# Linear-attention backward in a four-layer training step: feature derivative computed in place, and layer 0's key and value gradients transposed by DMA instead of TensorE

## The chip, the cores and the metric

The kernel runs on one core of a Trainium2 chip. The metric is the device time of one execution in microseconds (us), as the median of several executions. Before the change it is 2252.24 us, the median of 7 runs between 2244.93 and 2256.58 us. The profile below is of one further execution.

## What is computed

The reference is the forward pass and the gradients of four residual layers with sequence length 2048, width 640 and 32 heads of 20. Layers 0 and 2 are linear attention (A), layers 1 and 3 are sliding-window attention (B); the two A layers share their weights, and so do the two B layers. Cut to the part that the change touches:

```python
def _A_ref(x, wqkv, wo):                     # Dh = 20, H = 32
    qkv = (x @ wqkv).reshape(B, S, 3, H, Dh).transpose(2, 0, 3, 1, 4)
    q, k, v = qkv[0], qkv[1], qkv[2]
    phi = lambda t: jnp.where(t > 0, t + 1, jnp.exp(t)) + 1e-6
    pq, pk = phi(q), phi(k)
    kv = jnp.einsum("bhsd,bhse->bhde", pk, v)
    z = jnp.einsum("bhsd->bhd", pk)
    num = jnp.einsum("bhqd,bhde->bhqe", pq, kv)
    den = jnp.einsum("bhqd,bhd->bhq", pq, z)[..., None] + 1e-6
    o = num / den
    return o.transpose(0, 2, 1, 3).reshape(B, S, D) @ wo

x = x + _A_ref(_layernorm(x), A_wqkv, A_wo)
x = x + _B_ref(_layernorm(x), B_wqkv, B_wo)
x = x + _A_ref(_layernorm(x), A_wqkv, A_wo)
x = x + _B_ref(_layernorm(x), B_wqkv, B_wo)
_out, _vjp = jax.vjp(_f, A_x, A_wqkv, A_wo, B_wqkv, B_wo)
return (_out, *_vjp(grad_out))
```

The derivative of phi can be read off phi itself: for t > 0 it is 1, and for t <= 0 it is exp(t) = phi − 1e-6. So phi'(t) = min(phi − EPS, 1) with EPS = 1e-6. The backward pass keeps pq and pk from the forward pass and forms dq and dk by multiplying the gradient with respect to pq and pk by this derivative.

## The kernel before

The 2048 rows are worked on in 16 tiles of 128 rows (the partitions). Each tile has 640 columns, often taken as two halves of 320 (`CW`). The order of stages is: forward pass of the four layers; backward of layer 3's attention core; linear backward of layer 2 (about 1165 to 1285 us); backward of layer 1's core (to about 1750 us); then the weight gradients, which run to the end at 2253 us. The linear backward of layer 0 (about 1812 to 2037 us) is put amid the weight gradients.

The order of instructions on TensorE (PE), VectorE (DVE), ScalarE (ACT) and GpSimd (POOL) is the order in which the program issues them. It is written out by hand: each step of a tile has a slot number in the table `PLACES`, and all steps of all tiles are issued by rising slot. For the linear backward the list is `PLACES["l2"]`; tile t's step with offset a goes to slot 8t + a plus a base, so tiles follow each other at 8 slots. Layer 2 runs with nothing else in its slots but the ends of layer 3 and the beginning of layer 1. In layer 0 each slot ends with `fill(0.8)`, which issues some 0.8 us of weight-gradient matmuls. All DMAs are issued on SyncE's queue (SP), whose order the framework sets; at most 8 are under way, and an entry that waits for its data holds what stands behind it.

`plan_linear` (from L929) makes the steps of one tile. With their offsets:

- `load` (−10.4): for a pair of tiles, five DMAs, one of them `lpqk`, pq and pk beside one another (128 x 2 x 1280, bf16).
- `turn` dn (−1.3), v (0.6), pk (1.2): TensorE transposes the tile in six pieces of heads (`flip`, L162); DVE copies dn's result from PSUM (L167), ACT the others' (L165).
- `part`, two halves each of dn (1.9, 3.2), v (4.6, 6.2) and pk (7, 7.5): small products of the turned tile with the per-head matrices (L138) into a PSUM bank, `dense`. The result goes into `dqa`, a 128x1920 tile of dq, dk and dv. For dn (which gives dq) and v (which gives dk), DVE first computes `fd` = min(pq − EPS, 1), or that of pk, for 320 columns (L969), with one scalar_tensor_tensor and a constant tile `one`, and then multiplies the PSUM bank by it into dqa (L971). For pk (dv), ACT casts (L966).
- `turn_q` (5): dq is transposed into `dqT` by a DMA transpose (L978), in the first four tiles of layer 0 (`lp.by_pe` is 4 there, 0 in layer 2) by TensorE (`turn_pe`, L921).
- `turn_kv(1)` (8) and `turn_kv(2)` (8.3): dk and dv are transposed by five TensorE transposes each (L983); DVE copies dk's (L986), ACT dv's (L988) from PSUM to dqT. After the second, the whole of dqa is stored to `dqkv` in HBM; the weight gradients load it again as `rhs`.
- `dh(n, ci)` (10.2, 11.8, 14, 14.4, 15.4, 16): for each half ci, five products each of dqT's k, v and q part, in this order, with the transposed weights `WTA`, in one PSUM bank (`dense<-WTA,dqT`, L138); ACT then scales it into dh (L1001).
- `ln` (16.2) and `ln2` (18.7): layer norm backward: a DVE reduction (L1009), a small DVE op (L1011), an ACT op (L1018), and two POOL additions (L1012 with `lg`, L1019 into `lgn`). `lgn` is stored for each pair of tiles.

The weight gradients (`weight_jobs`, L1048 to L1110) keep a whole activation `lhs` (four DMA chunks of 640 KB) and slices of gradients `rhs` in SBUF; TensorE runs 32 matmuls per output piece (`wg`), which ACT (L1092) or DVE (L1094) casts to `wr`, stored by DMA. When the left operand changes, as late in the stage to `lhs<-o`, its chunks are loaded into buffers that have come free.

Of the kernel before, what the change touches and what calls it, by code (L numbers as in the profile page):

```python
# [11 lines left out]
ALU = mybir.AluOpType  # L12
AX = mybir.AxisListType
BF = mybir.dt.bfloat16
F32 = mybir.dt.float32
P = 128
D = 640
# [5 lines left out]
DT = D // P  # L23
# [10 lines left out]
CW = D // 2  # L34
LN_EPS = 1e-5
EPS = 1e-6
# [7 lines left out]
    f3=[-35.7, -30, -26.5, -25, -24, -23.8, -22.5, -18, -16.4, -14, -12.1, -7.4, -6.8, -6, -4.9, -3.5, -1.7, 11.3, 12.4, 13.4],  # L44
    bf=[2.1, 3.1, 5.2, 14.9, 17.9, 6.2, 7.8, 10, 14.6, 28.3],
    bh=[13.1, 14.5, 15.5, 17.1, 17.5, 18, 20, 21.2, 25.7, 28.3, 30, 36, 19.1, 20.1, 21.8, 22.5, 23.3, 24.6, 25.2, 27.5, 30.5, 31.7, 33, 35, 41.5, 43, 2.2, 8.3, 9.5, 12, 18.9, 34.5],
    l2=[-10.4, -1.3, 0.6, 1.2, 1.9, 3.2, 4.6, 6.2, 7, 7.5, 5, 8, 8.3, 10.2, 11.8, 14, 14.4, 15.4, 16, 16.2, 18.7],
    n1=[9.7, 0.5, 3.3, 3.6, 5.3, 9, 3, 4.7, 5.4, 5.6, 24],
    xx=[1, 1, 0, 0, 0, 0, 1, 1, 0, 0, 0, 0, 0, 1, 0, 0, 1, 0, 0, 0, 0, 0, 0, 1, 0, 0, 1, 0, 0, 0, 1, 0],
    bd=[0, 0, 1, 0, 0, 0, 1, 0, 0, 0, 0, 0, 0, 1, 1, 0, 0, 1, 1, 0, 1, 0, 1, 0, 1, 0, 1, 1, 0, 1, 1, 0])  # L50
# [2 lines left out]
class Kern:  # L53
    def __init__(self, ctx, tc, x0, A_w, A_wo, B_w, B_wo, grad, outs):
        self.ctx, self.tc = ctx, tc
        self.nc = nc = tc.nc
        self.W = dict(A=A_w, B=B_w)
        self.Wo = dict(A=A_wo, B=B_wo)
        self.grad = grad
        self.out_x4, self.out_gx, dWA, dWoA, dWB, dWoB = outs  # L60
        self.dW = dict(A=dWA, B=dWB)
        self.dWo = dict(A=dWoA, B=dWoB)
        self.serial = 0

        dram = ctx.enter_context(tc.tile_pool(name="dram", bufs=1, space=bass.MemoryType.DRAM))
        const = ctx.enter_context(tc.tile_pool(name="const", bufs=1))

        def d(name, shape, dt=BF):
            return dram.tile(shape, dt, name=name)

        self.hn = [d(f"hn{l}", [T, D]) for l in range(4)]
        self.dq = [d(f"dqkv{l}", [T, QT]) for l in range(4)]
        self.o = [d(f"o{l}", [T, D]) for l in range(4)]
        self.x2 = d("x2", [T, D])
        self.WTA, self.WoTB = d("WTAt", [P, NF * D]), d("WoTBt", [P, DT * D])
        self.x0 = x0
        self.gs = [d(f"g{l}", [T, D]) for l in range(3)] + [grad]
        self.sv = {}
        for l in (0, 2):
            self.sv[l] = dict(pqk=d(f"pqk{l}", [T, 2 * D]), v=d(f"v{l}", [T, DA]),  # L80
                              dn=d(f"dn{l}", [T, DA]))
        for l in (1, 3):
            self.sv[l] = {k: d(f"{k}{l}", [TT, P, 3, G * P]) for k in ("s", "T")}

        self.ident = const.tile([P, P], BF, name="ident")
        make_identity(nc, self.ident)
        self.bm = const.tile([KB, HB, HA], BF, name="bm")
        nc.gpsimd.memset(self.bm, 1.0)
        nc.gpsimd.affine_select(out=self.bm, in_=self.bm, compare_op=ALU.is_ge, fill=0.0, base=0,
                                pattern=[[-DH, HB], [0, HA]], channel_multiplier=1)  # L90
        nc.gpsimd.affine_select(out=self.bm, in_=self.bm, compare_op=ALU.is_ge, fill=0.0, base=DH - 1,
                                pattern=[[DH, HB], [0, HA]], channel_multiplier=-1)
        self.mhalf = const.tile([P, 1], F32, name="mhalf")
        nc.gpsimd.memset(self.mhalf, -0.5)
        self.rs = [const.tile([P, TT], F32, name=f"rs{l}") for l in range(4)]
        self.r = [const.tile([P, TT, H], F32, name=f"r{l}") for l in range(4)]
        self.mz = {l: const.tile([KB, 6, KA], BF, name=f"mz{l}") for l in (0, 2)}
        self.mzT = {l: const.tile([KA, 6, KB], BF, name=f"mzT{l}") for l in (0, 2)}
        self.one = const.tile([P, 1], BF, name="one")
        nc.gpsimd.memset(self.one, 1.0)  # L100
        self.dmz = const.tile([KB, 6, KA], BF, name="dmz")
        self.dmzT = const.tile([KA, 6, KB], BF, name="dmzT")
        self.macc = const.tile([KB, 6, KA], F32, name="macc")
# [823 lines left out]
    def plan_linear(self, st, lp, l, t, X, WT, g_out):  # L927

        nc = self.nc  # L929
        sv = self.sv[l]  # L930
        i = t % 2
        x = {}
# [9 lines left out]
        def src(nm):  # L942
            L = X[t // 2]
            return {"dn": L["dn"][:, i, :], "v": L["v"][:, i, :], "pq": L["pqk"][:, i, 0:D], "pk": L["pqk"][:, i, D:2 * D]}[nm]

        def turn(nm, K, cols, eng):
            x[nm] = self.flip(st.ps, lp.le, src(nm), nm + "T", K, 6, 0, eng, cols)

        def part(nm, c):
            if "dqkv" not in x:  # L950
                x["dqkv"] = lp.le.tile([P, QT], BF, name="dqa")
            tb, base = {"dn": (self.mzT[l], 0), "v": (self.dmzT, D), "pk": (None, 2 * D)}[nm]
            ps = st.ps.tile([P, 512], F32, name="dense", tag="m")
            jobs = []
            for h0, h1, j in ((0, 6, 0), (6, 12, 1), (12, 16, 2)) if c == 0 else ((16, 18, 2), (18, 24, 3), (24, 30, 4), (30, 32, 5)):
                out = ps[:, DH * (h0 - HALF * c):DH * (h1 - HALF * c)]
                if tb is not None:
                    rhs = tb[:, j, DH * (h0 - HS[j]):DH * (h1 - HS[j])]
                else:
                    rhs = self.dmz[:, j, :].rearrange("p (h d) -> p h d", d=HA)[:, h0 - HS[j]:h1 - HS[j], 0:DH]  # L960
                    out = self.heads(out)
                jobs.append((out, x[nm][:, j, :], rhs))
            self.banked(jobs)
            dst = x["dqkv"][:, base + c * CW:base + (c + 1) * CW]
            if nm == "pk":
                nc.scalar.copy(dst, ps[:, 0:CW])  # L966
            else:
                f = lp.le.tile([P, CW], BF, name="fd")
                nc.vector.scalar_tensor_tensor(out=f, in0=src("pq" if nm == "dn" else "pk")[:, c * CW:(c + 1) * CW], scalar=-EPS,  # L969
                                               in1=self.one.to_broadcast([P, CW]), op0=ALU.add, op1=ALU.min)  # L970
                nc.vector.tensor_tensor(out=dst, in0=ps[:, 0:CW], in1=f, op=ALU.mult)  # L971

        def turn_q():
            x["dT"] = st.sp.tile([P, NF, P], BF, name="dqT", bufs=3)
# [3 lines left out]
                self.dma(x["dT"][:, 0:DT, :], x["dqkv"][:, 0:D], transpose=True)  # L978

        def turn_kv(j):  # L980
            ps = st.ps.tile([P, 8, P], BF, name="flip", tag="m")
            for k in range(DT):
                nc.tensor.transpose(ps[:, k, :], x["dqkv"][:, j * D + k * P:j * D + (k + 1) * P], self.ident)  # L983
            o = x["dT"][:, j * DT:(j + 1) * DT, :]
            if j == 1:
                nc.vector.tensor_copy(o, ps[:, 0:DT, :])  # L986
            else:
                nc.scalar.copy(o, ps[:, 0:DT, :])  # L988
                self.dma(self.rows(self.dq[l], t), x["dqkv"])

        def dh(n, ci):
            if n == 0:
                x["ps"] = st.ps.tile([P, 512], F32, name="dense", tag="m")
                if ci == 0:
                    x["dh"] = st.sf.tile([P, D], F32, name="dh", tag="f")
                    x["ac"] = st.sm.tile([P, 2], F32, name="ac")
            k0 = (DT, 2 * DT, 0)[n]
            for k in range(k0, k0 + DT):
                self.mm(x["ps"][:, 0:CW], x["dT"][:, k, :], WT[:, k, ci * CW:(ci + 1) * CW], n == 0 and k == k0, n == 2 and k == k0 + DT - 1)
            if n == 2:  # L1000
                nc.scalar.activation(x["dh"][:, ci * CW:(ci + 1) * CW], x["ps"][:, 0:CW], ACT.Copy,  # L1001
                                     scale=self.rs[l][:, t:t + 1], accum_out=x["ac"][:, ci:ci + 1])
# [19 lines left out]
        a = PLACES["l2"]  # L1022
        fs = [lambda: turn("dn", KA, acols, nc.vector), lambda: turn("v", KA, acols, nc.scalar), lambda: turn("pk", KB, kcols, nc.scalar)]
        fs += [lambda nm=nm, c=c: part(nm, c) for nm in ("dn", "v", "pk") for c in range(2)]
        fs += [turn_q, lambda: turn_kv(1), lambda: turn_kv(2)]
        fs += [lambda n=n, ci=ci: dh(n, ci) for ci in range(2) for n in range(3)] + [ln, ln2]
        return ([(a[0], load)] if i == 0 else []) + list(zip(a[1:], fs))

    def linear_pools(self, left, side, by_pe):
# [382 lines left out]
```

The softmax here doesn't subtract the row's maximum and nothing guards it: scores larger than these inputs give would overflow.

## Time and profile before

| | |
|---|---|
| Median of 7 runs | 2252.24 us |
| Range of the runs | 2244.93 to 2256.58 us |
| Profiled execution, own time | 2254.7 us |
| Its span | 2253.0 us |
| Mean granted TensorE clock | 0.979 |
| Layer 2 tile period (starts of L1012) | 7.24 us |
| Layer 0 tile period (dqkv stores, 1863.43, 1876.57, ...) | 13.1 us |

The profile is of one execution. A group or timeline line names the source line, the engine, the operation and the result and inputs by the program's names, then the shapes; a bracket at the end of a timeline line tells how long the engine had been idle before it and what it waited for. "PEld" is the weight load of TensorE, which overlaps its matmuls, whose ends are modelled. In the chain of waits, each step is followed back to what released it. A row of the table of windows tells each engine's busy time in a stretch of the span. Rows of the page that give the setting, costliest groups of the two stages among them:

```profile
L138 PE MATMUL wg<-rhs,lhs 128*128 128x240 bf16 (+1 forms) x3840 | 375.3, 257 | 10.5 <-DMA lhs<-o 6.8
...
L1012 POOL TENSOR_TENSOR dh<-dh,lg 128x640 f32<-128x640 f32 x32 | 51.5, 1610 | 258.2 <-DVE s L1009 207.6
...
L138 PE MATMUL dense<-WTA,dqT 128*128 128x320 bf16 x960 | 161.5, 300 | 1.3 <-DMA dqT<-dqa 1.0
```

The columns after the shapes are the count, the busy time in us, the mean of one in ns, and the idle time before them with its main releaser. PE's idle time before the dh products in the whole span is 1.3 us, that before the weight gradients 10.5 us.

### The profile page before, as it was taken

The numbers are of one execution on the slowest core, as the hardware profiler recorded it, in microseconds if no ns is written. First come the engines' busy times: TensorE is split into PE (matmuls) and PEld (weight loads), VectorE is DVE, ScalarE is ACT, GpSimd is POOL, SyncE is SP. The second block draws the span as 40 slices with busy tenths as digits, with TensorE's granted clock in tenths as the row PEclk, the third lists the DMA queues.
The fourth block names the chain that finished last, engine by engine and source line by source line (L and its number), as shares of the span: only waits on it lengthen the run. The fifth ranks groups of instructions, "written<-read, shape, count | busy, mean of one in ns | idle before, by whom it ended". The sixth has DMA issues, their size and how long they took to land. (4 is left out here: it accounts for less than half of the span.)

```text
span 2253.0 us, 76829 instructions
## 1 busy us (share of the span) xinstructions
PE 2078.0 (92%) x32061; PEld 1693.0 (75%) x32061; DVE 1455.4 (65%) x2934; ACT 1356.7 (60%) x2109; POOL 1089.5 (48%) x1888
## 2 busy tenths in 40 slices
PE   7889998899989999998879899999998889999999
PEld 5667776577767877777767678777776788889998
DVE  6778885777744788887749858788776245550000
ACT  5467887377776888887736668788776234430000
POOL 2046665156666577777534456777774312220000
PEclk9999999999999999999989989999999999999999
DMA  7488875697879589998799733999987998857753
GB/s 260 141 238 227 226 223 150 165 222 218 206 210 230 150 182 209 210 215 178 164 280 260 200 88 106 199 207 211 198 191 165 270 290 244 255 161 199 201 143 90
DMA packets 721357, 449.50 MB, mean 200 GB/s; under 512 B 461296, under 2 KB 697840, under 8 KB 720624
## 3 DMA queue, kind: packets, MB, share of 16 engines
q1 hardware_dynamic: 721008, 444.58, 77.6%
q8 instruction: 251, 4.11, 0.8%
q14 instruction: 98, 0.80, 0.1%
HBM read 213.09 MB, written 149.82 MB: 161 GB/s over the span
## 5 line engine op out<-in xcount | busy, mean ns | idle before, releaser
L665 DVE TENSOR_TENSOR ds<-dp,e 128x768 bf16<-128x768 f32 (+2 forms) x512 | 464.1, 907 | 171.5 <-PE s L138 59.8
L662 ACT ACTIVATE e<-s 128x768 bf16<-128x768 f32 (+2 forms) x512 | 395.6, 773 | 138.0 <-PE s L138 102.7
L385 ACT ACTIVATE eT<-sT 128x1536 bf16<-128x1536 f32 (+2 forms) x256 | 350.8, 1370 | 131.5 <-PE sT L138 129.7
L138 PE MATMUL wg<-rhs,lhs 128*128 128x240 bf16 (+1 forms) x3840 | 375.3, 257 | 10.5 <-DMA lhs<-o 6.8
L138 PEld LDWEIGHTS <-lhs 128*128 128x128 bf16 x3840 | 338.1, 98 | 23.8 <-DMA lhs<-o 7.7
L674 POOL TENSOR_SCALAR_AFFINE_SELECT e<-e 128x256 bf16<-128x256 bf16 x512 | 207.2, 406 | 248.9 <-ACT e L662 244.1
L138 PEld LDWEIGHTS <-dqT 128*128 128x128 bf16 x1920 | 170.6, 98 | 62.9 <-issue 10.4
L391 POOL TENSOR_SCALAR_AFFINE_SELECT eT<-eT 128x512 bf16<-128x512 bf16 x256 | 162.2, 635 | 109.8 <-ACT eT L385 109.4
L138 PE MATMUL acc<-slabqs,ds 128*128 128x20 bf16 x2880 | 210.3, 172 | 1.4 <-ACT dq L744 0.5
L138 PE MATMUL dp<-slabvT,dT 32*128 32x384 bf16 (+2 forms) x1024 | 168.2, 321 | 45.0 <-DVE ds L665 39.8
L138 PE MATMUL acc<-ds,e 128*128 128x20 bf16 x2880 | 208.3, 172 | 0.0
L138 PEld LDWEIGHTS <-ds 128*128 128x128 bf16 x2880 | 187.9, 96 | 11.8 <-issue 3.5
L678 POOL TENSOR_SCALAR_AFFINE_SELECT e<-e 128x256 bf16<-128x256 bf16 x448 | 195.9, 437 | 0.0
L138 PEld LDWEIGHTS <-e 128*128 128x128 bf16 x2880 | 170.1, 96 | 10.6 <-issue 1.8
L1012 POOL TENSOR_TENSOR dh<-dh,lg 128x640 f32<-128x640 f32 x32 | 51.5, 1610 | 258.2 <-DVE s L1009 207.6
L685 PE MATMUL flip<-ident,ds 128*128 128x128 bf16 x1944 | 170.3, 222 | 3.3 <-DVE ds L772 1.2
L138 PE MATMUL s<-slabkT,slabqT 32*128 32x384 bf16 (+2 forms) x1024 | 168.2, 324 | 4.6 <-ACT dT L797 3.3
L1094 DVE CAST wr<-wg 128x240 bf16<-128x240 f32 (+1 forms) x72 | 27.2, 377 | 222.2 <-PE wg L138 219.9
L138 PE MATMUL dense<-WB,hnT 128*128 128x320 bf16 x960 | 166.2, 305 | 3.3 <-DVE o L459 2.2
L1092 ACT CAST wr<-wg 128x240 bf16<-128x240 f32 (+1 forms) x48 | 16.3, 339 | 254.0 <-PE wg L138 236.2
L138 PE MATMUL dense<-WTA,dqT 128*128 128x320 bf16 x960 | 161.5, 300 | 1.3 <-DMA dqT<-dqa 1.0
L138 PE MATMUL acc<-slabks,dsT 128*128 128x20 bf16 x2880 | 147.3, 172 | 10.8 <-DMA dsT<-ds 10.7
(176 smaller groups left out, 4606.4 us busy)
## 6 DMA issues: line engine op xcount, KB each, us to landing
rhs<-dqkv SPq DMA_DIRECT2D x64, 480.0 KB, 4.8
s<-s SPq DMA_DIRECT2D x32, 768.0 KB, 3.8
T<-T SPq DMA_DIRECT2D x32, 768.0 KB, 3.9
dqkv<-dq SPq DMA_DIRECT2D x16, 960.0 KB, 5.6
dqkv<-dqa SPq DMA_DIRECT2D x32, 480.0 KB, 4.6
slabkT<-T SPq DMA_DIRECT2D x56, 256.0 KB, 4.4
slabvT<-T SPq DMA_DIRECT2D x56, 256.0 KB, 3.7
slabks<-s SPq DMA_DIRECT2D x56, 256.0 KB, 3.7
```

Of the source, the lines that this page charges most:

```text
L138: return self.nc.tensor.matmul(out, lhsT=lhsT, rhs=rhs, start=start, stop=stop, skip_group_check=True, **kw)
L385: nc.scalar.activation(e[:, :, 0:nb * P], s[:, :, 0:nb * P], ACT.Exp)
L391: nc.gpsimd.affine_select(out=dg, in_=dg, compare_op=ALU.is_ge, fill=0.0, base=0, pattern=[[0, 4], [1, P]], channel_multiplier=-1)
L662: nc.scalar.activation(u.e[:, :, 0:u.cw], s[:, :, 0:u.cw], ACT.Exp)
L665: nc.vector.tensor_tensor(out=d.ds[:, :, 0:d.cw], in0=d.dp[:, :, 0:d.cw], in1=d.e[:, :, 0:d.cw], op=ALU.mult)
L674: nc.gpsimd.affine_select(out=dg, in_=dg, compare_op=ALU.is_ge, fill=0.0, base=0, pattern=[[0, 2], [-1, P]], channel_multiplier=1)
L678: nc.gpsimd.affine_select(out=fr, in_=fr, compare_op=ALU.is_ge, fill=0.0, base=-1, pattern=[[0, 2], [1, P]], channel_multiplier=-1)
L685: nc.tensor.transpose(ps[:, 3 * j + i, :], f.ds[:, j, i * P:(i + 1) * P], self.ident)
L1012: nc.gpsimd.tensor_tensor(out=x["dh"], in0=x["dh"], in1=L["g"][:, i, :], op=ALU.add)
L1092: nc.scalar.copy(o[:, 0:w], ps[:, 0:w])
L1094: nc.vector.tensor_copy(o[:, 0:w], ps[:, 0:w])
```

## The change

The constant `one` and the four `fd` ops per tile are gone. Instead two new steps per tile, `slope("pq")` at offset −2.3 and `slope("pk")` at offset 4.4, overwrite the loaded pq or pk of the tile (128x640, bf16) with min(x − EPS, 1) by one DVE tensor_scalar each; `part` then multiplies the PSUM bank by the overwritten tile directly. pq is read for nothing else here; pk's slope comes after its transposes at 1.2. This holds for both A layers: 128 `fd` ops go, 64 slopes come.

In layer 0 (`lp.by_pe` is 4), for tiles 4 to 15, `turn_kv` issues one DMA transpose of five 128x128 blocks for dk and one for dv on SP, in place of the ten TensorE transposes and the two copies; the store to `dqkv` is issued behind the second. For these tiles the offsets of the six dh steps, ln and ln2 are 5 larger. Layer 2 keeps its TensorE transposes. In the order of SP in layer 2, the transpose of dq of every other tile comes ahead of the load of lhn and the store of lgn; in layer 0 the new transposes stand among rhs and lhs loads and wr stores, and behind the last layer-0 tiles six chunks of `lhs<-o` instead of five are behind the wr store at 2063 us.

```diff
-        self.one = const.tile([P, 1], BF, name="one")
-        nc.gpsimd.memset(self.one, 1.0)
...
-    l2=[-10.4, -1.3, 0.6, 1.2, 1.9, 3.2, 4.6, 6.2, 7, 7.5, 5, 8, 8.3, 10.2, 11.8, 14, 14.4, 15.4, 16, 16.2, 18.7],
+    l2=[-10.4, -1.3, 0.6, 1.2, 1.9, 3.2, 4.6, 6.2, 7, 7.5, 5, 8, 8.3, 10.2, 11.8, 14, 14.4, 15.4, 16, 16.2, 18.7, -2.3, 4.4],
...
             if nm == "pk":
                 nc.scalar.copy(dst, ps[:, 0:CW])
             else:
-                f = lp.le.tile([P, CW], BF, name="fd")
-                nc.vector.scalar_tensor_tensor(out=f, in0=src("pq" if nm == "dn" else "pk")[:, c * CW:(c + 1) * CW], scalar=-EPS,
-                                               in1=self.one.to_broadcast([P, CW]), op0=ALU.add, op1=ALU.min)
-                nc.vector.tensor_tensor(out=dst, in0=ps[:, 0:CW], in1=f, op=ALU.mult)
+                nc.vector.tensor_tensor(out=dst, in0=ps[:, 0:CW], in1=src("pq" if nm == "dn" else "pk")[:, c * CW:(c + 1) * CW], op=ALU.mult)
+
+        def slope(nm):
+
+            nc.vector.tensor_scalar(out=src(nm), in0=src(nm), scalar1=-EPS, scalar2=1.0, op0=ALU.add, op1=ALU.min)
...
         def turn_kv(j):
+            if lp.by_pe and t >= 4:
+                self.dma(x["dT"][:, j * DT:(j + 1) * DT, :], x["dqkv"][:, j * D:(j + 1) * D], transpose=True)
+                if j == 2:
+                    self.dma(self.rows(self.dq[l], t), x["dqkv"])
+                return
...
-        fs += [lambda n=n, ci=ci: dh(n, ci) for ci in range(2) for n in range(3)] + [ln, ln2]
+        fs += [lambda n=n, ci=ci: dh(n, ci) for ci in range(2) for n in range(3)] + [ln, ln2, lambda: slope("pq"), lambda: slope("pk")]
+        if lp.by_pe and t >= 4:
+            a = a[:13] + [v + 5 for v in a[13:21]] + a[21:]
         return ([(a[0], load)] if i == 0 else []) + list(zip(a[1:], fs))
```

## The prediction

> **What bounds the kernel now.** I read the page first, then the chain of waits, then each stage that the edit touches in a table of windows, then one tile of it on the timeline. The page's totals and the chain by engine:
>
> ```profile
> PE 2078.0 (92%) x32061; PEld 1693.0 (75%) x32061; DVE 1455.4 (65%) x2934; ACT 1356.7 (60%) x2109; POOL 1089.5 (48%) x1888
> ...
> PE 20%; DMA 2%; SPq 1%; DVE 0%; ACT 0%; issue 0%; DVEq 0%; ACTq 0%
> ```
>
> TensorE (PE) is busy 92% of the span, and VectorE (DVE) hardly stands in the chain. But this edit touches only the two linear backward passes, so these decide. A row below gives the start, the length and the busy time of each engine, then the granted clock, the DMA share and GB/s: first layer 2, then layer 0 amid weight gradients, then the full-queue moment behind it.
>
> ```profile
> 1168.00:1283.00 115.00, 106.79 (x1219) 86.06 (x1219) 104.39 (x202) 75.50 (x152) 45.72 (x32) 0.96 0.82 229
> 1863.00:2035.00 172.00, 172.00 (x1849) 152.98 (x1847) 92.06 (x178) 67.24 (x141) 40.35 (x27) 1.00 0.74 209
> 2066.00:2074.00 8.00, 8.00 (x88) 7.70 (x87) 0.81 (x2) 0.36 (x1) 0.00 (x0) 1.00 1.06 368
> ```
>
> In layer 2 DVE is as full as PE (104.4 and 106.8 of 115 us). In layer 0 PE never stops (172.0 of 172.0; ends of matmuls are modelled, but no idle time stands before any of its groups there) and DVE is half idle: there an edit pays only if it takes work off PE. One layer-2 tile (start, duration, what; PE first, then DVE, then POOL) shows who waits for whom:
>
> ```profile
> 1229.58 0.84 PE L138 MATMUL dense<-WTA,dqT 128*128 128x320 bf16 x5
> 1230.85 0.32 PE L138 MATMUL dense<-dmz,pkT 120*128 120x40 bf16 x4 [0.43 <-DVE dqa L971]
> ```
> ```profile
> 1226.29 0.48 DVE L969 SCALAR_TENSOR_TENSOR fd<-lpqk,one 128x320 bf16<-128x320 bf16 x1
> 1226.86 0.49 DVE L971 TENSOR_TENSOR dqa<-dense,fd 128x320 bf16<-128x320 f32 x1
> 1227.27 1.11 DVE L969 SCALAR_TENSOR_TENSOR fd<-lpqk,one 128x320 bf16<-128x320 bf16 x1
> 1228.48 0.49 DVE L971 TENSOR_TENSOR dqa<-dense,fd 128x320 bf16<-128x320 f32 x1
> 1228.89 1.32 DVE L969 SCALAR_TENSOR_TENSOR fd<-lpqk,one 128x320 bf16<-128x320 bf16 x1
> ```
> ```profile
> 1226.32 1.70 POOL L1012 TENSOR_TENSOR dh<-dh,lg 128x640 f32<-128x640 f32 x1 [3.69 <-DVE s L1009]
> 1228.32 1.54 POOL L1019 TENSOR_TENSOR lgn<-dh,lna 128x640 bf16<-128x640 f32 x1 [0.29 <-POOL dh L1012]
> ```
>
> PE runs the tile back to back except once, where the next product needs a PSUM bank that DVE's dqa (L971) has not emptied. Groups of five dh products follow at 0.68 us, so this one should be through at 1230.26; the next work starts at 1230.85: 0.59 us lost. DVE is late because fd (L969) takes 0.48 us by itself but 1.11 and 1.32 us while POOL adds dh and lgn.
>
> **Part one, the derivative in place.** Removed per tile: four fd of 320 columns, 0.48+1.11+1.32+0.48 = 3.39 us of DVE. Added: two slopes of 640 columns (bf16, SBUF to SBUF, one input). No such op stands in these stages. Nearest rows: the in-place TENSOR_SCALAR of half the width in the forward pass (L560: minimum 230, median 244, maximum 666 ns) and the full-width one (L417 hn<-xm: 436, 441, 741 ns). I take 0.44, the full-width row, with 0.35 and, beside POOL, 2 us as ends. The four products keep 0.49 us: with PSUM as one input they took that next to POOL too. What stays on DVE per tile is 4×0.49 + dnT 0.55 + k's copy 0.49 + L1009 and L1011 1.1 = 4.1 us: before 4.1 + 3.39 = 7.5 (a few tenths of it overlap: the tile takes 7.24), after 4.1 + 2×0.44 = 5.0 us.
>
> Here a rule matters. The Trainium skill (SBUF — State Buffer, "Who interferes with whom") says that VectorE and GpSimd share one port pair under an exclusive lock, so that an op that uses the shared port waits for the whole op that holds it. fd's rows agree (0.48 alone, 1.11 and 1.32 under POOL ops of 1.70 and 1.54). It speaks against the change, since a fast one-input op in SBUF is also said to take the shared pair, and the maxima 666 and 741 ns hint at it. By the median row DVE needs 5.0 us per tile; if both slopes had to sit out a POOL op, 5.0 + 1.7 + 1.5 = 8.2 and nothing would be won. Two full waits are improbable: POOL is busy 3.2 of 7.2 us and its two ops follow one another right behind L1009, in the time of the dq parts; the slopes' slots (2.3 ahead of the tile, and 4.4) put them at other places, at least one outside. One wait of 1.5 makes 6.5, still under PE's 6.64 below. I take that: no DVE bound.
>
> What is late next is PE itself. One tile period is 7.24 us (L1012 starts from 1182.87 to 1284.29, 14 periods); less the 0.59 hole, PE has 6.64 us of work. ACT is busy 5.6 and POOL 3.2 us per tile. Some wait will stay: a turned q by DMA comes late twice (1.0 us in all now), so 6.69: gain 0.55×14 = 7.7 us. Ends: 8.4 (no hole left), 5 (half a slope wait surfaces). Pq's slope stands ahead of its tile; lpqk was issued some 12 us before it and lands in 4.9 to 6.5 us, so DVE waits for nothing new. SP's order changes only in that alternate q transposes pass the lhn load and lgn store: nothing there waits for them.
>
> In layer 0 the same removal is hidden under a full PE, with one exception, at its start, where no weight gradients fill in (start, duration, idle before):
>
> ```profile
> 1845.17 1.54 DVE L969 SCALAR_TENSOR_TENSOR fd<-lpqk,one 128x320 bf16<-128x320 bf16 x1
> ...
> 1847.36 0.34 PE L921 MATMUL flip<-ident,dqa 128*128 128x128 bf16 x3 [1.76 <-DVE dqa L971]
> ```
>
> This fd is in the chain of waits ("DVE fd L969 0%"); it goes, the slope having run earlier: 1.5 us, ends 0 and 2.
>
> **Part two, k and v turned by DMA (12 tiles of layer 0).** Removed per tile: ten PE transposes, one DVE copy (0.49 us) and one ACT copy; the latter two are hidden. Added: two DMA transposes of five blocks, with their issue on SP.
>
> ```profile
> 1864.28 0.72 PE L983 MATMUL flip<-ident,dqa 128*128 128x128 bf16 x10
> 1864.84 0.51 PE L162 MATMUL flip<-ident,lv 128*126 128x128 bf16 x6
> ```
>
> 1864.84 − 1864.28 = 0.56 us of a PE that never stops: 12×0.56 = 6.7 us. The Trainium skill (VectorE: DVE Perf Modes, "The three transpose paths" and "Rules for kernel authors") gives 390 ns for a 128×128 transpose by TensorE and 1309 ns by the DMA path, and says to use TensorE if PSUM will do: against this change. By its figures ten PE transposes would be worth 3.9 us per tile and ten DMA ones 13; by the rows 0.56 us back to back, and one DMA transpose of five blocks takes 1.25 us of SP (1.21 to 2.56) and lands after 3.6 us (2.6 to 6.3). I go by the rows. What counts is which resource has room: PE none, the DMA engines a quarter (share 0.74). An isolated one cost about 0.87 us of all 16 engines, so two per 13.1 us tile bring 0.74 to about 0.87.
>
> Does dh then wait? Turned at slots 8 and 8.3, k is first read at 10.2+5 = 15.2: 7 slots of about 1.64 us, 11.8 us. Needed: two issues of 1.25 and a landing of 3.6 = 6.1; worst seen 2×2.56+6.3 = 11.4. It fits, unless the entries ahead on SP are themselves waiting: the rhs and lhs loads, the wr stores (for ACT's L1092 cast), lg and lhn (for POOL L1012 and ACT's L1018) hold what is behind them. Tile 4 is tightest (about 8 us of PE work between). I charge nothing and keep 1 us per tile as the bad end. Moving dh, ln and ln2 by 5 slots lengthens the tail of the last tile; weight gradients stand behind it and fill PE.
>
> One cost I charge: after layer 0 PE waits for `lhs<-o`, a 640 KB chunk, 1.83 us at 2076.31, with the queue full (share 1.06, 368 GB/s). Five such chunks stand there behind a wr store now, six after. 640 KB at 368 GB/s is 1.75 us. Ends 0 and 3.5.
>
> Sum for layer 0: 6.7 + 1.5 − 1.75 = 6.5 us; ends 2 and 9. Altogether 7.7 + 6.5 = 14.2 us: the profiled execution (2254.7, span 2253.0) would come to 2240.5, and the median of the runs, 2.5 lower, to 2238.0.
>
> **Rivals.**
> - Only layer 2 gains. PE's freed 6.7 us come back as dh waits of some 0.3 us per tile and a longer lhs hole. For: SP would carry 24 entries more in a stage whose queue already held PE up at its end. Against: 11.8 us of room, share 0.74. Time: 2252.2 − 7.7 = 2244.5.
> - Only layer 0 gains: the slopes take fd's place as waiters for POOL and DVE stays at 7 us per tile. For: the maxima 666 and 741. Against: half as many ops, one input, POOL idle most of the tile. Time: 2252.2 − 6.5 − 1 = 2244.7.
> - The change doesn't do what it says: PE's hole is set by something other than DVE, and layer 0's PE pays the same in later waits. The hole is named DVE dqa eleven times in 1180 to 1290 (4.9 us, longest 0.5), with no other engine near it. Time: 2251.
> - Slower: the k and v transposes stand in SP behind an entry that waits (lg for POOL, lhn for ACT, wr for its cast) and reach dh late in every tile. The point is 11.8 us from slot 8 to slot 15.2; with 1.5 for that entry, 2×2.56 issue and a landing of 6.3, each at its worst, it is 12.9, 1.1 late per tile: 13 us, which about cancels the gain; with an entry held 3.5 us, 3.1 late, 37 us lost, 2275. From 1.2 us per tile on the change loses. For: in layer 0 lhs and rhs loads come in bursts (slices of the window at 370 GB/s). Against: each term is the slowest seen, not the usual one.
>
> **How the numbers follow.** Both gains near size: 0.60, at 2238 (2232 to 2242). Only one of them: 0.24, at 2244.6 (2241 to 2248). Nothing: 0.09, at 2251. Slower: 0.07, about 2259 to 2275. The range, 2231 to 2249, leaves out the last two cases and a little below. A measurement of this kernel can tell about 0.2%, 4.5 us, from no change. The second case lies at 7.6 us, mostly beyond that: faster 0.83, within 0.10, slower 0.07.
>
> **What would show it.** Layer 2: L1012 starts 6.7 us apart instead of 7.24, DVE busy some seven tenths of the stage instead of nine, no PE wait for dqa, PE near full; slopes near 0.44 us, none over 2. Layer 0: PE 240 rows fewer, period about 12.6 us instead of 13.15, no "PE dense <- DMA dqT<-dqa" wait to speak of, dqT landing at 3.6. The hole before `lhs<-o` at 3 to 4 us. I am wrong if the slopes' mean in layer 2 is over 1.5 us, if the period stays at 7.2, or if dh waits for dqT by more than 0.5 us per tile.

## The result and the profile after

The changed kernel takes 2236.38 us, the median of 12 runs (2227.67 to 2243.36), beside 2252.25 us of 31 runs before; the ratio is 0.9929, 95% interval 0.9916 to 0.9942, a gain of 16.0 us (13.1 to 18.9). Forecast were 2238.0 us. The profiled execution took 2235.65 us, its span 2233.9 at a mean granted clock of 0.980.

The page's totals and chain of the changed kernel (line numbers are two to six off those of before: fd and dqa's L971 is now L966, the slopes are L970, L983 is L987, L1009 and L1012 are L1013 and L1016):

```profile
PE 2067.6 (93%) x31941; PEld 1685.6 (75%) x31941; DVE 1390.2 (62%) x2858; ACT 1349.8 (60%) x2097; POOL 1084.0 (49%) x1887
...
PE 19%; DMA 2%; SPq 1%; DVE 0%; ACT 0%; issue 0%; DVEq 0%; ACTq 0%
```

The stages, in the table of windows of the changed kernel: layer 2, then 135 us of layer 0.

```profile
1170.00:1275.00 105.00, 102.09 (x1226) 84.22 (x1224) 83.72 (x170) 75.24 (x153) 41.58 (x32) 0.99 0.92 250
...
1855.00:1990.00 135.00, 135.00 (x1434) 119.80 (x1432) 45.57 (x119) 50.85 (x105) 30.60 (x20) 1.00 1.03 256
```

In layer 2 PE is now busy 97% of the stretch and DVE 80%, where they stood at 93 and 91. In layer 0 PE is full as before, and the DMA share has gone to 1.03. The same length of layer 0 before was:

```profile
1868.00:2003.00 135.00, 135.00 (x1470) 120.34 (x1468) 78.34 (x148) 52.66 (x109) 32.14 (x21) 1.00 0.81 225
```

One layer-2 tile of the changed kernel, PE where the hole was, then DVE's slopes and products, then POOL:

```profile
1226.94 0.84 PE L136 MATMUL dense<-WTA,dqT 128*128 128x320 bf16 x5
1227.62 0.32 PE L136 MATMUL dense<-dmz,pkT 120*128 120x40 bf16 x4
```
```profile
1224.70 0.62 DVE L970 TENSOR_SCALAR lpqk<-lpqk 128x640 bf16<-128x640 bf16 x1
1225.43 0.49 DVE L966 TENSOR_TENSOR dqa<-dense,lpqk 128x320 bf16<-128x320 f32 x1
1225.84 1.56 DVE L970 TENSOR_SCALAR lpqk<-lpqk 128x640 bf16<-128x640 bf16 x1
1227.32 0.48 DVE L966 TENSOR_TENSOR dqa<-dense,lpqk 128x320 bf16<-128x320 f32 x1
```
```profile
1223.74 1.40 POOL L1016 TENSOR_TENSOR dh<-dh,lg 128x640 f32<-128x640 f32 x1 [2.76 <-DVE s L1013]
1225.68 1.54 POOL L1023 TENSOR_TENSOR lgn<-dh,lna 128x640 bf16<-128x640 f32 x1 [0.54 <-POOL dh L1016]
```

The product follows the group of five at 0.68 us (1226.94 to 1227.62), so the 0.59 us hole is closed. L1016 starts 6.58 us apart in most tiles, 6.64 in the mean of fourteen. The two slopes take 0.62 and 1.56 us, and each ends 0.18 us after an op of POOL does (at 1225.14 and 1227.22): they do sit POOL out, as fd did, and it costs nothing because DVE has room.

Set side by side by stages (each difference of two starts in a profile; "layer 2" from the first to the last POOL dh op, "weight stage" from the end of the last hole before the first `lhs<-o` to the end of the last hole before the late `lhs<-o`; the last column sums the late holes):

| profile | layer 2 | weight stage | late lhs<-o hole |
|---|---|---|---|
| before | 112.77 | 299.66 | 1.83 |
| changed | 104.25 | 291.17 | 3.47 |
| changed, second profile | 105.04 | 294.37 | 4.20 |
| part one alone | 104.15 | 297.55 | 1.75 |
| part two alone, two profiles | 113.05, 113.22 | 292.68, 295.47 | 3.58, 3.97 |
| tile 15 by TensorE, two profiles | 103.84, 103.64 | 289.29, 291.56 | 1.29, 1.50 |

In the first profile 8.5 us come from layer 2 and 8.5 from the weight stage, 17.0 in all. Not all of the weight stage's share belongs to the change. About 5.6 us lie where it acts: 6.05 us less work of TensorE and 1.15 us less of a hole at layer 0's start, against 1.64 us more of late holes. The other 3 us lie ahead of that start, in the same instructions: TensorE waited there for loads of rhs for 3.70 us before and for 1.90 after (0.75 in the second profile), and the rest of that stretch took 66.2 and 65.0 us at granted clocks of 0.95 and 0.97. No run ties these to the edit.

The two profiled executions lie 19.1 us apart. The stretch between the two stages, layer 1's core, was 4.4 us shorter as well (481.0 against 476.7 us from layer 2's last POOL dh op to the start of the weight stage), though its instructions are the same; what stands ahead of layer 2 and behind the late hole was 0.6 and 1.6 us longer. Over the profiles of this study layer 1's core took 476.1 to 481.0 us in the four of kernels with fd and 473.7 to 478.9 in the ten with slopes. The two sets overlap and lean apart; whether the change has a small part in it stays open.

### The profile page after: what moved, and what is told of

Read it like the earlier page. It is cut to its first block, busy times and chain, and to the rows that moved or that the text cites. A ratio compares the mean times of both kernels' runs of the same rounds, so it can differ in the third digit from the quotient of the medians.

```text
span 2233.9 us, 76495 instructions
## 1 busy us (share of the span) xinstructions
PE 2067.6 (93%) x31941; PEld 1685.6 (75%) x31941; DVE 1390.2 (62%) x2858; ACT 1349.8 (60%) x2097; POOL 1084.0 (49%) x1887
## 5 line engine op out<-in xcount | busy, mean ns | idle before, releaser
L136 PEld LDWEIGHTS <-lhs 128*128 128x128 bf16 x3840 | 339.0, 98 | 26.5 <-DMA lhs<-o 10.4
L136 PEld LDWEIGHTS <-dqT 128*128 128x128 bf16 x1920 | 170.6, 98 | 62.1 <-issue 10.4
L1016 POOL TENSOR_TENSOR dh<-dh,lg 128x640 f32<-128x640 f32 x32 | 46.0, 1437 | 235.4 <-DVE s L1013 227.2
```

The source lines that it names most:

```text
L136: return self.nc.tensor.matmul(out, lhsT=lhsT, rhs=rhs, start=start, stop=stop, skip_group_check=True, **kw)
L1016: nc.gpsimd.tensor_tensor(out=x["dh"], in0=x["dh"], in1=L["g"][:, i, :], op=ALU.add)
```

## The experiments

**slope_only: part one alone.** The changed kernel without its new branch and without the shift:

```diff
-            if lp.by_pe and t >= 4:
-                self.dma(x["dT"][:, j * DT:(j + 1) * DT, :], x["dqkv"][:, j * D:(j + 1) * D], transpose=True)
...
-        if lp.by_pe and t >= 4:
-            a = a[:13] + [v + 5 for v in a[13:21]] + a[21:]
```

> Part one alone: slopes in place in both layers, layer 0's k and v turned by TensorE as before. My theory (the two parts add up; layer 2 is worth 8.0 us, the start of layer 0 2.8): 2252.2 - 10.8 = 2241.4, ratio 0.995; L1012's starts 6.58 us apart in layer 2, layer 0's tiles 13.1 us apart, hole before lhs<-o at 1.8 us. Rival (part two is worth nothing, and the whole gain of the changed kernel is part one's): 2236.4, ratio 0.993.

Measured: 2243.74 us, ratio 0.9958 (0.9940 to 0.9976), a gain of 9.5 us (5.4 to 13.5). Layer 2 in 104.15 us, layer 0's tiles 13.14 us apart, the hole 1.75 us. So part one gives the whole of layer 2's gain and leaves the rest to part two; the rival's 2236.4 lies below the interval.

**dma_only and dma_again: part two alone**, the new branch and the shift added to the kernel before:

```diff
+            if lp.by_pe and t >= 4:
+                self.dma(x["dT"][:, j * DT:(j + 1) * DT, :], x["dqkv"][:, j * D:(j + 1) * D], transpose=True)
...
+        if lp.by_pe and t >= 4:
+            a = a[:13] + [v + 5 for v in a[13:21]] + a[21:]
```

> Part two alone: fd as before, layer 0's k and v of tiles 4 to 15 turned by DMA with the later dh slots. My theory: 12 x 0.56 us of TensorE gained, 1.7 us given back as a longer hole before lhs<-o: 2252.2 - 5.0 = 2247.2, ratio 0.998; layer 0's tiles 12.6 us apart, layer 2's 7.24. Rival (the transposes' waits and DMA load eat it): 2252, tiles at 13.1 us.

Measured: 2252.89 us, ratio 0.9994 (0.9981 to 1.0008): by the median the rival was right. By the profile it was not: layer 0's tiles stood 12.6 us apart, no TensorE wait for dqT stood in them, and the weight stage was 7.0 us shorter. In this profile the gain was lost ahead of that: the first POOL dh of layer 2 came at 1190.25 us, not at 1182.87, in a stretch whose instructions are those of before, with a granted clock of 0.97 from 900 to 1100 us against 0.99. So the same kernel was run again:

> Part two alone once more. Its weight-gradient stage was 7.0 us shorter in the profile, but its median only 0.3 us below before's, at a mean granted clock of 0.9767 against 0.9784. Theory (the clock was lower by chance, in stages that the edit doesn't touch): this time 2245 to 2249, with a clock nearer 0.978. Rival (part two by itself costs some us elsewhere or draws a lower clock each time): 2251 to 2254 again, clock 0.977 or less.

Measured: 2247.80 us of 22 runs, ratio 0.9987 (0.9977 to 0.9997), a gain of 2.9 us (0.7 to 5.2), at a mean clock of 0.9784. The first series' ratio is a gain of 1.4 us (−1.8 to 4.3), so the two agree. An average of both, weighted by their intervals, is some 2.3 us (0.5 to 4.2): small, and below my 5.0. The clock as the cause isn't settled. It was 0.9767 in the first series and 0.9784 in the second, beside 0.9784 and 0.9791 for the kernel before in the same series, lower both times, while the changed kernel's was 0.9797 and 0.9795.

**fd_form: the same fd, in place and size, with one input.**

```diff
-                nc.vector.scalar_tensor_tensor(out=f, in0=src("pq" if nm == "dn" else "pk")[:, c * CW:(c + 1) * CW], scalar=-EPS,
-                                               in1=self.one.to_broadcast([P, CW]), op0=ALU.add, op1=ALU.min)
+                nc.vector.tensor_scalar(out=f, in0=src("pq" if nm == "dn" else "pk")[:, c * CW:(c + 1) * CW], scalar1=-EPS,
+                                        scalar2=1.0, op0=ALU.add, op1=ALU.min)
```

> The kernel before with one thing changed: fd is computed at the same four places and in the same size, but by a tensor_scalar with one input in place of the scalar_tensor_tensor with two. My theory (fd is long because it stands beside POOL's ops and sits them out, so that its place and its count matter, the form less): some fd still over 1 us, mean 0.5 to 0.65 us in place of 0.85, DVE frees 0.8 to 1.4 us per tile; since only 0.6 us were missing, most of the hole may close: period 6.6 to 6.9, time 2243 to 2248. Rival (the two-input form alone is at fault): every fd at 0.2 us, period 6.58, 2241.5. Second rival (the wait for POOL is just as long): period 7.1 or more, 2250 to 2252.

Measured: 2246.73 us, ratio 0.9969 (0.9958 to 0.9980), period 6.93 us. Two fd of a tile and the hole, on DVE and PE:

```profile
1218.00 1.50 DVE L969 TENSOR_SCALAR fd<-lpqk 128x320 bf16<-128x320 bf16 x1
...
1220.02 0.23 DVE L969 TENSOR_SCALAR fd<-lpqk 128x320 bf16<-128x320 bf16 x1
```
```profile
1219.12 0.84 PE L138 MATMUL dense<-WTA,dqT 128*128 128x320 bf16 x5
1220.15 0.32 PE L138 MATMUL dense<-dmz,pkT 120*128 120x40 bf16 x4 [0.19 <-DVE dqa L971]
```

Alone the one-input op takes 0.23 us instead of 0.48, but beside POOL it takes up to 1.5 us as before; its mean in layer 2 is 0.69 us, a little above what I expected. Counted as before, from 0.68 us behind the start of the group of five, the hole goes from 0.59 to 0.35 us, and the period from 7.24 to 6.93 on the way to 6.58. So the form alone closes somewhat less than half of it; the rest goes with the slopes' halved count and earlier place, which no run parts. Neither rival holds alone.

**slope_twice: how much room DVE has.**

```diff
             nc.vector.tensor_scalar(out=src(nm), in0=src(nm), scalar1=-EPS, scalar2=1.0, op0=ALU.add, op1=ALU.min)
+            nc.vector.tensor_scalar(out=src(nm), in0=src(nm), scalar1=0.0, scalar2=1.0, op0=ALU.add, op1=ALU.min)
```

> The changed kernel with every slope followed by a second one of the same form that leaves the values as they are (min(x + 0, 1)). It measures DVE's slack in layer 2. Theory (DVE has 5.2 of 6.57 us per tile, a second pair adds 0.64 alone, and up to 1.9 where it stands beside POOL): 5.9 to 7.1 us, so mostly hidden: period 6.57 to 6.9, time 2236 to 2241. Rival (DVE is as good as full already, each us of it shows): 1.3 us per tile on the period, 7.9, 2254.

Measured: 2240.72 us of 4 runs, ratio 0.9951 (0.9935 to 0.9967); layer 2 took 104.30 us, as without the second slope, at DVE's busy share of 88% (79.45 of 90 us from 1185 on). So DVE is not the bound of the changed layer 2, and work of DVE put there shows nothing in that stage's length. The median a little above the changed kernel's isn't explained by a stage; the mean clock of the four runs was 0.977, beside 0.980.

**no_shift: DMA turn without the five slots.**

```diff
-        if lp.by_pe and t >= 4:
-            a = a[:13] + [v + 5 for v in a[13:21]] + a[21:]
```

> The changed kernel without the five slots more for dh, ln and ln2: k's DMA transpose is issued 2.2 slots (some 3.5 us of TensorE work) ahead of its reader, v's 3.5 slots (5.5 us). My theory (room is what makes the DMA turn free; a transpose needs 1.25 us of issue and 4.1 us of landing, the second one 1.25 more, and what stands ahead on SP): TensorE waits 2 to 3.5 us in each of 12 tiles, time 2260 to 2278. Rival (the shift isn't needed, since the queue is quick enough or other work is issued in between): 2236 to 2240.

Measured: 2245.45 us, ratio 0.9961 (0.9948 to 0.9973). Some 9 us worse than the changed kernel, so the shift is needed; but I had expected 24 to 42. TensorE waited for dqT five times, 6.5 us in all, the first of the DMA tiles worst. A tile in the middle shows why so little: DVE's last product of dk, SP's transpose, and the readers (DVE, SP, PE):

```profile
1864.70 1.24 PE L136 MATMUL dense<-WTA,dqT 128*128 128x320 bf16 x5 [3.43 <-DMA dqT<-dqa]
...
1904.74 0.85 PE L136 MATMUL dense<-WTA,dqT 128*128 128x320 bf16 x5
1906.85 0.85 PE L136 MATMUL dense<-WTA,dqT 128*128 128x320 bf16 x5 [0.29 <-DMA dqT<-dqa]
```
```profile
1898.01 0.49 DVE L966 TENSOR_TENSOR dqa<-dense,lpqk 128x320 bf16<-128x320 f32 x1 [1.75 <-PE dense L136]
```
```profile
1898.53 1.21 SPq L106 DMA_TRANSPOSE dqT<-dqa  x1
```

SP's order isn't tied to the slots of the compute engines. The transpose starts as soon as dk is written (1898.50), at slot 6.2 and not at 8, and the reader comes 6.2 us later. The room is counted from the data. That also corrects my 11.8 us for the changed kernel: from the end of dk's last product to the reader it is 12.4 us in most of its tiles (10.4 to 13.3).

**shift3: three slots instead of five.**

```diff
-            a = a[:13] + [v + 5 for v in a[13:21]] + a[21:]
+            a = a[:13] + [v + 3 for v in a[13:21]] + a[21:]
```

> The changed kernel with dh, ln and ln2 moved by 3 slots in place of 5. With 0 slots TensorE waited 7.2 us in all for dqT and for lna in the 12 tiles, not the 24 to 42 that I had expected. Theory (room in front of the reader is what counts, and 3 slots, some 4.7 us more, cover nearly every landing up to 8.2 us): waits under 2 us in all, time 2235 to 2238. Rival (a few transposes are held on SP for longer than any such shift): waits of 3 us or more remain, 2239 to 2243.

Measured: 2239.56 us of 6 runs, ratio 0.9944 (0.9927 to 0.9961). By the median this is in the rival's range; by the profile it isn't: a single wait of 0.41 us for dqT is left, not 3 us, and the weight stage of 292.55 us lies between the two profiles of five slots. So three slots are nearly enough, and what makes the median some 3 us higher than the changed kernel's isn't shown (the intervals of the two ratios overlap).

**kv_l2: the DMA turn in layer 2 too.**

```diff
-            if lp.by_pe and t >= 4:
+            if not lp.by_pe or t >= 4:
...
-        if lp.by_pe and t >= 4:
+        if not lp.by_pe or t >= 4:
```

> The changed kernel with layer 2's k and v turned by DMA as well (all 16 tiles, dh, ln and ln2 five slots later there too). Theory: the DMA turn was cheap in layer 0 because the DMA engines had room there (share 0.81 before, 1.03 after). In layer 2 they have none: share 0.92 at a period of 6.58 us, and two transposes of about 0.87 us of all engines each would add 0.26, to 1.18. TensorE then waits for dqT or for loads, period 7.0 to 7.6 us, 6 to 14 us slower than the changed kernel: 2242 to 2250. Rival (TensorE is the bound, DVE has room, and the DMA load is elastic): 0.56 us per tile gained, period 6.0, 2228.

Measured: 2266.76 us, ratio 1.0066 (1.0047 to 1.0086), slower than before the change. Layer 2 took 127.59 us, 23.3 more than in the changed kernel. The window and PE's waits in layer 2 (what is waited for, us in all, times, longest):

```profile
1175.00:1275.00 100.00, 82.98 (x832) 66.10 (x832) 48.55 (x123) 50.64 (x107) 32.50 (x25) 0.89 1.02 252
```
```profile
PE dense L136 <- DMA dqT<-dqa: 19.0, 8, 3.6
```

The direction is the theory's, the size is not: 30 us over the changed kernel against 6 to 14. DVE has half its time free and PE a sixth. Tiles come 6.2 to 11.4 us apart (between 1188 and 1316), and the granted clock fell to 0.89, which the forecast didn't have. The same edit that gained in layer 0 costs 30 us here.

The theory's cause, full DMA engines, is not what the trace shows for most of the wait. The transposes land no later than those of q do in the changed kernel's layer 2 (median 3.7 us, longest 6.6, against 4.2 and 7.1), and the changed kernel's layer 0 runs at a share of 1.03 without one such wait. But in every second tile k's transpose starts late. One such tile, in DVE (dk's last product), POOL, SP and PE:

```profile
1229.62 0.48 DVE L966 TENSOR_TENSOR dqa<-dense,lpqk 128x320 bf16<-128x320 f32 x1
```
```profile
1229.42 1.54 POOL L1016 TENSOR_TENSOR dh<-dh,lg 128x640 f32<-128x640 f32 x1 [4.90 <-DVE s L1013]
1231.04 1.54 POOL L1023 TENSOR_TENSOR lgn<-dh,lna 128x640 bf16<-128x640 f32 x1
```
```profile
1230.98 0.36 SPq L106 DMA_DIRECT2D lg<-g  x1
1231.44 0.42 SPq L106 DMA_DIRECT2D lhn<-hn  x1
1232.61 0.36 SPq L106 DMA_DIRECT2D g<-lgn  x1
1233.07 3.84 SPq L106 DMA_TRANSPOSE dqT<-dqa  x2
```
```profile
1238.11 1.28 PE L136 MATMUL dense<-WTA,dqT 128*128 128x320 bf16 x5 [3.46 <-DMA dqT<-dqa]
```

dk is written at 1230.10. On SP the load of lg stands ahead of its transpose until POOL's first op ends (1230.96), and the store of lgn until POOL's second ends (1232.58), so it starts 3.0 us late. PE was ready for it at 1234.65, 4.6 us after dk; it landed at 1238.06. Five of the eight waits, 15.0 of the 19.0 us, are of this kind, with 3.0 to 3.6 us of holding. This is the mechanism of the prediction's slower rival, in layer 2. It is read from the trace; no run took the hold away.

**last_pe and last_again: tile 15 turned by TensorE, unshifted.**

```diff
-            if lp.by_pe and t >= 4:
+            if lp.by_pe and 4 <= t < TT - 1:
...
-        if lp.by_pe and t >= 4:
+        if lp.by_pe and 4 <= t < TT - 1:
```

> The changed kernel with the last tile (15) of layer 0 turned by TensorE and not shifted, as before the change; tiles 4 to 14 by DMA. Theory (the longer hole before lhs<-o comes from the last tile's later end, which puts one chunk more behind the wr store on SP): five chunks there again, hole back from 3.5 to about 1.8 us, 0.5 us of transposes paid: 1.1 us better than the changed kernel, 2235.2. Rival (the hole is of other making): hole 3.5 us, 0.5 us worse, 2236.9. The time can hardly tell these apart; the hole can.

Measured: 2234.06 us, ratio 0.9925 (0.9910 to 0.9940). SP again has three `lhs<-o` chunks early and five behind the wr store, as before the change; the changed kernel had two and six. The holes, in the kernel before, in the changed one and in this one:

```profile
2076.31 3.91 PE L138 MATMUL wg<-rhs,lhs 128*128 128x160 bf16 x54 [1.83 <-DMA lhs<-o]
```
```profile
2052.01 0.45 PE L136 MATMUL wg<-rhs,lhs 128*128 128x160 bf16 x4 [0.81 <-DMA lhs<-o]
2053.83 0.45 PE L136 MATMUL wg<-rhs,lhs 128*128 128x160 bf16 x4 [1.37 <-DMA lhs<-o]
2055.56 24.62 PE L136 MATMUL wg<-rhs,lhs 128*128 128x160 bf16 x330 [1.29 <-DMA lhs<-o]
```
```profile
2056.14 24.04 PE L136 MATMUL wg<-rhs,lhs 128*128 128x160 bf16 x345 [1.29 <-DMA lhs<-o]
```

1.83, then 0.81 + 1.37 + 1.29 = 3.47, then 1.29 us: the one more chunk is the hole's growth. Once more, beside the changed kernel on one chip:

> The kernel of last_pe once more, beside the changed kernel on the same chip. Theory: 1 to 2 us better than the changed kernel, by the shorter hole before lhs<-o. Rival: the same, or worse by the 0.5 us of TensorE transposes.

> The changed kernel once more, for a second profile and for comparison on one chip: 2236 to 2237. In its profile layer 2 from the first to the last L1012 at 104.2 us, and the hole before lhs<-o at 3.5 us; the other stages may differ by some us from the first profile (as layer 1's core did, 4 us, at a lower granted clock) though nothing in them has changed.

Measured: 2231.52 us against the changed kernel's 2234.97, ratios to before 0.9921 (0.9907 to 0.9934) and 0.9934 (0.9921 to 0.9948). Both pairs lean the same way, by 2.3 and 3.5 us in the medians and by 0.9 and 2.9 in the ratios; the intervals overlap, so the time alone doesn't prove it.

**dqa3: a third buffer for dqa**, on top of last_pe:

```diff
-                x["dqkv"] = lp.le.tile([P, QT], BF, name="dqa")
+                x["dqkv"] = lp.le.tile([P, QT], BF, name="dqa", bufs=3)
...
-            x[nm] = self.flip(st.ps, lp.le, src(nm), nm + "T", K, 6, 0, eng, cols)
+            x[nm] = self.flip(st.ps, lp.le, src(nm), nm + "T", K, 6, 0, eng, cols, **(dict(bufs=1) if nm == "pk" else {}))
```

> Tile 15 turned by TensorE as in last_pe, and dqa with three buffers in place of two (the turned pk with one in place of two, to make room), so that the third layer-0 tile need not wait for the dqkv store of the first. It tests what is left of the hole at layer 0's start, where TensorE waits 1.7 to 2.6 us for dqa behind DVE's wait for DMA dqkv<-dqa. Theory (that store is what DVE waits for): the hole goes, 1.5 to 2.5 us better than last_pe beside it, some 2232. Rival (with the store's wait gone DVE waits for lpqk's load, or pk's single buffer holds TensorE up in layer 2): no gain, 2234 to 2240.

Measured: 2230.46 us, ratio 0.9915 (0.9900 to 0.9930), the fastest kernel of the study. In the changed kernel layer 0 still starts with a hole, of DVE behind the store of dqa and of PE behind DVE:

```profile
1830.07 0.89 DVE L966 TENSOR_TENSOR dqa<-dense,lpqk 128x320 bf16<-128x320 f32 x2 [2.51 <-DMA dqkv<-dqa]
```
```profile
1830.62 0.74 PE L919 MATMUL flip<-ident,dqa 128*128 128x128 bf16 x5 [1.69 <-DVE dqa L966]
```

The third buffer is paid for with one of the turned pk's two. With it neither wait is there, and nothing of the kind has taken its place but one wait of 0.49 us for dqT. The weight stage took 288.17 us, with 1.83 us of holes at `lhs<-o`. Against last_again it is 1.1 us in the medians, less than the runs can tell apart.

## Why the prediction held, point by point

**The bound.** "In layer 2 DVE is as full as PE", and PE the next to be late: shown. The hole closed, and doubling the slopes moved nothing.

**The slope's price.** I took 0.44 us from the full-width row; alone it takes 0.32 (median 0.322, minimum 0.315). Beside POOL I expected at least one of a tile's two outside; in layer 2 both mostly stand beside POOL's ops (0.62 and 1.56 us above, mean 0.96). DVE's time per tile came to 83.7/105 × 6.58 = 5.2 us, between my 5.0 and 6.5, and its share to 80% where I had some seven tenths. The rule of the port pair that I weighed against the change is what the rows show (a one-input op does sit POOL out). It didn't matter because the sum stayed under PE's, as forecast for one wait of a tile's two; that the slopes' place would keep one outside was wrong in most tiles.

**Layer 2: 7.7 us.** Measured 8.5 and 7.7 in two profiles, 8.6 with part one alone. An undisturbed period is 6.58, where I had 6.64 for PE's work: closing the hole gave 0.66 us per tile, not 0.59. With the late tiles the mean is 6.64, against my 6.69; PE's waits for the transposed q were 0.8 us in all in the first profile and 1.6 in the second, about the 1.0 of before.

**Layer 0's start: 1.5 us.** This term was too high. "This fd ... goes, the slope having run earlier": so it did, but DVE's product also waited for the dqkv store, and that wait stood in the trace of before, on the line just ahead of the fd:

```profile
1844.76 0.49 DVE L971 TENSOR_TENSOR dqa<-dense,fd 128x320 bf16<-128x320 f32 x1 [1.50 <-DMA dqkv<-dqa]
```

PE's two holes there were 2.84 us together before; in one they are 1.69 (changed), 2.04 (part one alone) and 2.88 (changed, second profile). The gain is 0 to 1.2 us, by the store's landing. dqa3 took that store's wait away and the hole with it.

**k and v by DMA: 6.7 us.** From one dh group behind the start of layer 0, the same in both kernels (before, then changed), to the late hole:

```profile
1849.55 0.84 PE L138 MATMUL dense<-WTA,dqT 128*128 128x320 bf16 x5
```
```profile
1833.21 0.84 PE L136 MATMUL dense<-WTA,dqT 128*128 128x320 bf16 x5
```

With the holes left out, that stretch took 224.9 us before and with part one alone, 218.9 changed and with part two alone. That is 6.05 us, 0.50 per tile instead of 0.56. Landing rose from 3.6 to 4.1 us (longest from 6.3 to 8.2), within the room of 12.4. That I charged nothing for entries ahead on SP came out right, but not because none of them waits. In one tile of the changed kernel (DVE writes dk, SP, PE reads):

```profile
1893.61 0.48 DVE L966 TENSOR_TENSOR dqa<-dense,lpqk 128x320 bf16<-128x320 f32 x1
```
```profile
1894.97 0.36 SPq L106 DMA_DIRECT2D lg<-g  x1
1896.18 0.36 SPq L106 DMA_DIRECT2D lhn<-hn  x1
1897.85 0.38 SPq L106 DMA_DIRECT2D out_dram<-lgn  x1
1898.32 2.69 SPq L106 DMA_TRANSPOSE dqT<-dqa  x2
```
```profile
1906.48 0.84 PE L136 MATMUL dense<-WTA,dqT 128*128 128x320 bf16 x5
```

k's transpose is held for 4.2 us, more than any hold I had reckoned with, and lands at 1902.0; the five slots cover it. The DMA load was mis-sized: I had 0.74 to 0.87, the rows show 0.81 to 1.03 in 135 us of full tiles. By 1.03 × 12.6 − 0.81 × 13.1 that is an estimated 2.4 us of all engines per tile, not 1.75, so about 1.2 us for a transpose here, where I had 0.87 from an isolated one.

**The longer hole: −1.75 us.** Measured −1.64 (1.83 to 3.47), −2.37 in the second profile; last_pe shows its cause.

**Sum and rivals.** 14.2 us forecast, 16.0 (13.1 to 18.9) measured, 14.9 (11.7 to 17.8) in the second series. Where the change acts, the first profile gives 8.5 and 5.6, 14.1 us, and the second 7.7 and 3.2. That the sum comes so near is in part luck: layer 2 was forecast too low, layer 0's start and the transposes too high. "Only layer 2 gains" (2244.5) is what part one alone gives, 2243.7; the changed kernel is well below. The slower rival had its point at 11.8 us of room, which is 12.4 counted from the data; no_shift, with 6 to 7 us in most tiles, loses part two's gain and little more. In layer 2, with 4.6 us of room in most of the tiles that wait, the same turn does make the kernel slower than before.

**What stays open.** The changed kernel's gain is 16.0 us, the parts alone give 9.5 and 2.9 (0.7 to 5.2), 12.4 in all. The intervals bridge it. The stages in single profiles add up too (8.6 + 2.1 + 7.0 = 17.7 against 17.0), but 1.7 and 1.8 us of the 2.1 and 7.0 are shorter waits for rhs ahead of layer 0, and the weight stage of one and the same kernel differs by 2 to 3 us between profiles, by its DMA holes and the clock. Whether something small gains only with both parts, or in layer 1's core, can't be told from these runs.

## What to carry to other kernels

Look for the engine that is late at the one hole in a steady tile, and sum its work per tile with and without the edit: a slowdown by a neighbour (here POOL) is harmless as long as the sum stays under the next bound. Moving transposes from TensorE to DMA pays where TensorE is full and the time from data to reader covers both the landing and what holds the DMA queue ahead of them: with 12.4 us it did, with 4.6 us the same edit cost 30 us. Where a step moves later at the end of a stage, look for the loads that wait for its buffers: here one tile given back to TensorE, for 0.5 us, took 2.2 us off the holes.

## What the runs showed of the hardware that was not expected

- The in-place tensor_scalar of 128x640 with constants takes 0.32 us, the one with per-row scalars in the forward pass (L417, not in place) 0.44 us at the same size and type; which of the two differences counts isn't tested.
- POOL gains too: its dh addition (L1012, then L1016) went from a mean of 1610 ns to 1437 over the 32 tiles, 1.70 to 1.40 us in the tiles shown. In layer 2 the means are 1666 ns before, 1448 with the one-input fd and 1399 with slopes, so most of it goes with fd's form.
- The granted clock differs from run to run and goes with the time: in the 12 runs of the changed kernel 0.976 to 0.984, from 2243.36 us at 0.976 to 2230.74 at 0.984, though not strictly (the fastest, 2227.67, had 0.982). In kv_l2's layer 2, with its eight waits of TensorE, it was 0.89, beside 0.99 in the changed kernel; whether the waits lower it isn't tested.
- A DMA that waits on SP holds the transposes behind it though their data is there: 3.0 us in kv_l2's tile and 4.2 us in the changed kernel's, shown above.
